# Attention and a mixture of experts in one kernel: products with V in two visits per head pair, full-array forms, and a reordered step table

## The chip, the cores and the metric

One core of a Trainium2 chip runs the whole program. The metric is the device time in microseconds of one execution. The matrix engine is called PE below (its weight loads PEld), the vector engine DVE, the scalar engine ACT, the general engine POOL, and SP issues most of the DMAs.

## The reference, cut to what matters

```python
q_rot, k_rot = rotate(q), rotate(k)                 # q, k, v: 2 batches, 8 heads, 576 tokens, 64 wide
scores = q_rot @ k_rot^T / sqrt(64)
attn = softmax(scores)                              # max subtracted; sum + 1e-9 below
x = (attn @ v) -> [1152, 512]                       # tokens by heads
logits = x @ w_gate; expert = argmax(logits)        # 8 experts, each with a capacity of 288 tokens
y = gate * relu(x_e @ w1[e]) @ w2[e]                # zero for a token that found no room
out = prelu(y @ w_in) @ w_out
```

All of it is float32.

## The kernel before

The program is one hand-ordered stream (a manual schedule): each engine runs its instructions in the order in which the code calls them, and waits are set by semaphores between engines. A step that stands late in one engine's queue cannot pass a step that stands before it.

Attention works on eight head pairs `j` (two heads of one batch each). The 576 tokens of a pair are four tiles of 128 and one rest of 64. Nine softmax steps make a pair: `(t, hh)` for four tiles and two heads, and `(4, 0)` for the two rests together. The loop `for n in range(10, ...)` counts slots, ten to a pair, so that `j, s = divmod(n, 10)`; one slot of the ten, `SCH["none"]`, has no softmax step. In each slot the letters of `SCH["seq"]` = `SATXPR` are gone through in order:

- **S**, `S_step`: the logits of a step (4 products, 8 for the rests; K is split in a high and a low half, so two stationary operands), into one of two `pss` buffers in PSUM; then DVE takes the row maximum (`nm`, line 308), and ACT the exponential into `P` (line 309), with the row sums in `ss`.
- **T**, `T_step`, two slots later (`lag`): PE transposes `P` into `pt` (and `pr`, which stays open for a pair), ACT or DVE (by the table `SCH["e"]`) copies it to `PT` and `PR`.
- **A**, `AV_steps(j - 1)`: the products of the former pair's `PT` and `PR` with `v`. Both heads have 64 columns, and each has its own half of the array's columns (a 128x64 form). Two halves of the tokens by five blocks of keys are ten pieces, one piece (two products, four records in the trace) in each slot. After five pieces the result is copied to `oT`.
- **X**, `xl_steps(j - 2)`: PE multiplies `oT` by `G` (an identity and the gate's weights), tile by tile, which gives tokens by features and the gate's logits; DVE scales both by the inverse row sums `ri` and writes `x_tok` and `lp`. The fifth tile has 64 columns, so it too is a 128x64 form.
- **P**, `prep_T`, `prep_rem`, `prep_X` for pair `j + 1`: PE transposes `hl` (K and Q of each head in two halves) into `pT`; a copy by DVE (K) or ACT (Q) makes `T`. `prep_rem` does so for the rests (`rb`, from the 64 rows of `remhl` that hold this batch: a form of 64 rows). `prep_X` issues two DMAs that swap halves of `T`.
- **R** for pair `j + 2`: `ropeA` on POOL (three operations for K, three for Q), `remA` (three), `ropeB` and `remB`: a cast on ACT and then a subtraction on POOL, which end in `hl` and `remhl`.

All of A, T, X and P take their PSUM tiles from one pool `ps1` with four buffers. After the letters come the slot's loads (`SCH["load"]`) and `hook(n)`, which starts the routing of the first batch at slot 53 (DVE, a few small products on PE, five indirect DMAs on POOL), `choose` at 61, the first expert's weights at 66, their splitting (ACT, POOL) from 68, and `make_xT` from 81. The last pair's products with V have the slots 80 to 89 to themselves, and its `xl_steps` come at 86 and 90. After that the expert and the feed-forward stages run.

Of the kernel before, what the change touches and what calls it, by code (L numbers as in the profile page):

```python
# [12 lines left out]
F32 = mybir.dt.float32  # L13
# [11 lines left out]
P = 128  # L25
# [20 lines left out]
SCALE = 1.0 / math.sqrt(D)  # L46
BIG = float(1 << 20)
LEFT, RIGHT = "left", "right"
SCH = {'xl': [0, 2], 'T': [1, 1, 1, 2], 'rem': 3, 'X': 4, 'rope': [0, 0, 7, 9, 3, 9], 'load': 9, 'none': 9, 'lag': 2, 'seq': 'SATXPR', 'e': [1, 1, 0, 0, 1, 0, 1, 0, 0, 0, 1, 0, 0, 0, 1, 0, 0, 0, 1]}


def rope_tables():
# [11 lines left out]
def attention(nc, tc, q, k, v, wg, tab, rtab, x_tok, lp, ident, idr, hook):  # L64
# [3 lines left out]
    with ExitStack() as ctx:  # L68
# [14 lines left out]
        vrem = cp.tile([P, 2, 8, 64], F32, name="vrem")  # L83
        G = cp.tile([P, 4, 144], F32, name="G")
        TR = cp.tile([P, 2, 3, 64], F32R, name="TR")
        nc.vector.memset(TR[:, :, 1].bitcast(F32), 0.0)
        state = {}

# [109 lines left out]
        def prep_rem(j):  # L198


            b, hp = divmod(j, NPAIR)
            h0 = 2 * hp
            st = state[j]
            rb = ps1.tile([P, 4, 64], F32R, tag="ps1", name=f"rb_{j}")
            sl = slice(64 * b, 64 * b + 64)
            for i in range(2):
                for hh in range(2):
                    nc.tensor.transpose(
                        rb[:, i * 2 + hh, :],
                        remhl[sl, i, h0 + hh].rearrange("p two d -> p (two d)"),  # L210
                        idr[sl, sl],
                    )
            flat = T_of(j, 1).rearrange("p h n -> p (h n)")[:, 512:640].rearrange("p (h n) -> p h n", h=2)
            for i, o in ((1, flat), (0, TR[:, j % 2, 0:3:2])):
                move(nc.scalar, i, o, rb[:, 2 * i : 2 * i + 2, :].bitcast(F32))
            st["X"] = pT.tile([P, 2, 576], F32R, tag="X", name=f"X_{j}")

        def prep_X(j, hh=None):
# [133 lines left out]
        def AV_steps(j):  # L352
            b, hp = divmod(j, NPAIR)
            st = state[j]
            PT, PR = st["PT"], st["PR"]
            oT = p2.tile([P, 576], F32, tag="oT", name=f"oT_{j}")
            st["oT"] = oT
            for half in range(2):
                ps = ps1.tile([P, 512], F32, tag="ps1", name=f"av_{j}_{half}")
                for kb in range(5):  # L360
                    for hh in range(2):
                        lhs = st["v"][:, hh, kb, :] if kb < 4 else vrem[:, b, 2 * hp + hh, :]
                        nc.tensor.matmul(  # L363
                            ps[64 * hh : 64 * hh + 64, 0:288],
                            lhsT=lhs,
                            rhs=(PT[:, hh, kb] if kb < 4 else PR)[:, half * 288 : half * 288 + 288],
                            start=(kb == 0),
                            stop=(kb == 4),
                        )
                    if kb == 4:  # L370
                        copy(17 + half, oT[:, half * 288 : half * 288 + 288], ps[:, 0:288])
                    yield

        def xl_steps(j, parts=((0, 3), (3, 5))):
            b, hp = divmod(j, NPAIR)
            st = state[j]
            oT = st["oT"]
            ri = p2.tile([P, 5, 2], F32, tag="ri", name=f"ri_{j}")
            nc.vector.tensor_scalar(ri, st["ssum"], 1e-9, None, op0=ALU.add)
            nc.vector.reciprocal(ri, ri)  # L380
            nc.vector.tensor_copy(ri[0:64, 4, 1:2], ri[64:128, 4, 0:1])
            for t0, t1 in parts:
                ps = ps1.tile([P, t1 - t0, 144], F32, tag="ps1", name=f"xl_{j}_{t0}")
                for t in range(t0, t1):
                    m = 128 if t < 4 else 64
                    nc.tensor.matmul(
                        ps[:m, t - t0, :], lhsT=oT[:, t * 128 : t * 128 + m], rhs=G[:, hp, :], start=True, stop=True
                    )
                last, later = j == B * NPAIR - 1 and t1 == 5, []
                for a, e, m in ((t0, min(t1, 4), 128), (4, t1, 64)):  # L390
                    if a >= e:
                        continue
                    rb = lambda n: ri[:m, a:e, :].unsqueeze(3).broadcast_to([m, e - a, 2, n])
                    src = ps[:m, a - t0 : e - t0]
                    nc.vector.tensor_tensor(
                        lp[:m, b, a:e, 2 * hp : 2 * hp + 2, :],
                        src[:, :, 128:144].rearrange("p t (h d) -> p t h d", h=2),
                        rb(8),
                        op=ALU.mult,
                    )  # L400
                    xo = x_tok[:m, b, a:e, hp * 128 : hp * 128 + 128].rearrange("p t (h d) -> p t h d", h=2)
                    xi = src[:, :, 0:128].rearrange("p t (h d) -> p t h d", h=2)
                    if not last:
                        nc.vector.tensor_tensor(xo, xi, rb(64), op=ALU.mult)
                        continue
                    later += [(xo[:, t - a, h], xi[:, t - a, h], ri[:m, t, h : h + 1]) for t in range(a, e) for h in range(2)]
                for xo, xi, scale in later:
                    nc.scalar.activation(xo, xi, AF.Copy, scale=scale)
                yield
            state.pop(j)  # L410
# [93 lines left out]
        for n in range(10, len(steps) + 11):  # L504
            j, s = divmod(n, 10)
            for what in SCH["seq"]:
                if what == "S" and n < len(steps):
                    if steps[n][1]:
                        S_step(j, *steps[n][1])
                if what == "T" and 0 <= n - LAG < len(steps):  # L510
                    jt, x = steps[n - LAG]
                    if x:
                        T_step(jt, *x)
                if what == "A" and 1 <= j <= NJ:
                    if s == 0:
                        avg = AV_steps(j - 1)
                    next(avg)
                if what == "X":
                    xs0 = SCH["xl"] if j < NJ else (1, 2)
                    if j >= 2 and s in xs0:  # L520
                        if s == xs0[0]:
                            xlg = xl_steps(j - 2)
                        next(xlg)
                if what == "P" and j + 1 < NJ:
                    for i, (x, y) in enumerate(zip(SCH["T"], ((1, 0), (1, 1), (0, 0), (0, 1)))):
                        if s == x:
                            prep_T(j + 1, *y, eng(i))
                    if s == SCH["rem"]:
                        prep_rem(j + 1)
                    if s == SCH["X"]:  # L530
                        prep_X(j + 1)
                        prep_sums(j + 1)
                if what == "R" and j + 2 < NJ:
                    at = SCH["rope"]
                    if s == at[0]:
                        ropeA(j + 2, Q, 1)
                    if s == at[1]:
                        ropeA(j + 2, Q, 0)
                    if s == at[4]:
                        remA(j + 2, Q)  # L540
                    if s == at[2]:
                        ropeB(j + 2, Q, 1)
                    if s == at[3]:
                        ropeB(j + 2, Q, 0)
                    if s == at[5]:
                        remB(j + 2, Q)
            if n in (NJ * 10 + 6, NJ * 10 + 10):
                if s:
                    xlg = xl_steps(NJ - 1, ((0, 2), (2, 5)))
                next(xlg)  # L550
            if s == SCH["load"] and j + 3 < NJ:
                prep_load(j + 3)
            if j == 1 and s == 4:
                for hh in range(2):
                    nc.sync.dma_start(
                        G[64 * hh : 64 * hh + 64, :, 128 + 8 * hh : 136 + 8 * hh],
                        wg.rearrange("(c hh p) e -> hh p c e", hh=2, p=64)[hh],
                    )
            if n == 10 * (NJ - 1) - 5:
                prep_ctx.close()  # L560
            hook(n, ps1)
# [284 lines left out]
def build(nc, tc, cap, q, k, v, wg, w1, w2, w_in, w_out, alpha, tab, rtab, out):  # L846
    assert 0 < cap <= W
    with ExitStack() as top:
# [110 lines left out]
        def hook(n, psum):  # L959
# [11 lines left out]
                nc.vector.tensor_scalar(nal, al, -1.0, None, op0=ALU.mult)  # L971
            if n > 16 and fill:
                nc.sync.dma_start(fill.pop(0), zero[0:96].unsqueeze(1).broadcast_to([96, 3, 512]))
            if n == 53:
                hook.r = gate.route(0, psum, "ps1")
            if n in (53, 54, 55, 56):
                next(hook.r)
            if n == 61:
                hook.c = gate.choose()
# [651 lines left out]
```

## Time and profile before

| | |
|---|---|
| time, median of 3 runs | 464.43 us (464.12 to 465.53) |
| the profiled execution: its own time | 468.51 us |
| its span, first to last instruction | 466.7 us |
| PE busy | 421.9 us (90% of the span) |
| DVE, ACT, POOL busy | 305.5, 216.1, 238.7 us |
| granted PE clock, mean | 0.982 |

A busy time is the union of an engine's instructions. Matmuls overlap in the array's pipeline, so what one costs is read from the distance between the starts of neighbours, not from its own duration. "[0.57 <-DVE nm L308]" behind an instruction says that its engine sat idle 0.57 us before it, and that line 308's `nm` on DVE ended that wait. "x4" stands for four instructions that were merged into one row.

### The profile page before, as it was taken

To read this page: it belongs to the slowest core of one execution; us is meant where nothing else is said; L and a number is where in the kernel's file an instruction comes from. 1 tells how busy PE (TensorE), PEld (TensorE's weight loads), DVE (VectorE), ACT (ScalarE), POOL (GpSimd) and SP (SyncE) were. 2 spreads that over 40 slices of the span, in tenths; PEclk is the share of its full clock that TensorE was granted. 3 is DMA by queue.
4 is the path that set the end of the run, shared out by engine and by line. 5 is a ranking of instruction groups with operands and counts; after the bars stand their busy time and mean duration, and the time that the engine had idled before them with its cause. 6 is when DMAs were issued, how large, how long until landed. Compare 5 with 4: busy or idle time off the path is not lost. (4 is left out here: it accounts for less than half of the span.)

```text
span 466.7 us, 8223 instructions
## 1 busy us (share of the span) xinstructions
PE 421.9 (90%) x2993; PEld 332.2 (71%) x2993; DVE 305.5 (65%) x563; ACT 216.1 (46%) x540; POOL 238.7 (51%) x280
## 2 busy tenths in 40 slices
PE   6789999999989999995878798998999899889993
PEld 3576666666666666695867798697689589758962
DVE  8996566574777464579489911139888797886321
ACT  2476767666665667342253331164424514432600
POOL 6578482864775334148645310047736745662532
PEclk9999999999999999999899898999999999999998
DMA  7422999604031624467466667940314045000012
GB/s 215 129 60 48 175 332 295 185 1 121 0 119 35 195 88 160 158 228 250 104 208 216 235 222 264 374 170 1 122 60 180 5 178 183 0 1 0 2 69 73
DMA packets 37329, 63.71 MB, mean 137 GB/s; under 512 B 9886, under 2 KB 16158, under 8 KB 37280
## 3 DMA queue, kind: packets, MB, share of 16 engines
q1 hardware_dynamic: 35424, 58.83, 39.7%
q0 software_dynamic: 1568, 3.95, 2.3%
q8 instruction: 25, 0.41, 0.4%
q10 hardware_dynamic: 288, 0.33, 0.2%
q14 instruction: 24, 0.20, 0.1%
HBM read 47.35 MB, written 11.65 MB: 126 GB/s over the span
## 5 line engine op out<-in xcount | busy, mean ns | idle before, releaser
L308 DVE TENSOR_REDUCE nm<-S 128x1 f32<-128x576 f32 x72 | 54.2, 755 | 45.0 <-PE S L299 27.7
L309 ACT ACTIVATE P<-S,nm 128x576 f32<-128x576 f32 x72 | 53.5, 742 | 52.6 <-DVE nm L308 51.0
L1124 PE MATMUL u_a<-yh,whl 128*128 128x256 f32 (+1 forms) x576 | 71.3, 284 | 6.1 <-ACT room L1134 5.7
L1124 PEld LDWEIGHTS u_a<-yh,whl 128*128 128x128 f32 x576 | 70.1, 188 | 7.4 <-ACT room L1134 6.4
L1136 DVE SCALAR_TENSOR_TENSOR room<-room,nal 128x256 f32<-128x256 f32 (+1 forms) x48 | 30.5, 637 | 30.9 <-ACT room L1134 30.8
L330 PEld LDWEIGHTS pt<-ident,P 128*128 128x128 f32 x256 | 27.0, 141 | 29.3 <-ACT P L309 6.8
L1026 POOL TENSOR_TENSOR whl<-wraw,whl 128x512 fp32r<-128x512 f32 x22 | 28.9, 1312 | 35.8 <-ACT whl L1025 32.7
L363 PE MATMUL av<-PT,v 128*64 128x288 f32 x256 | 44.7, 431 | 0.4 <-DVE PT L319 0.3
L1188 PE MATMUL acc<-whl,split_room 128*128 128x512 f32 x162 | 42.3, 396 | 2.2 <-DVE xs L1200 1.2
L330 PE MATMUL pt<-ident,P 128*128 128x128 f32 x256 | 41.5, 286 | 3.1 <-ACT P L309 2.9
L1025 ACT CAST whl<-wraw 128x512 fp32r<-128x512 f32 x22 | 14.5, 657 | 54.2 <-DVE wraw L1022 54.2
L1188 PEld LDWEIGHTS acc<-whl,split_room 128*128 128x128 f32 x162 | 29.7, 188 | 13.1 <-DVE xs L1200 2.9
L1142 POOL TENSOR_TENSOR g<-room,g 128x272 fp32r<-128x272 f32 (+2 forms) x21 | 17.7, 853 | 41.7 <-ACT g L1141 39.2
L299 PE MATMUL S<-T,T 128*128 128x288 f32 x112 | 36.1, 338 | 1.1 <-DVE T L178 1.1
L1188 PE MATMUL acc<-whl,g 128*128 128x512 f32 x126 | 32.9, 391 | 0.5 <-POOL whl L1026 0.5
L299 PE MATMUL S<-X,T 128*128 128x288 f32 x112 | 31.2, 293 | 0.0
L154 POOL TENSOR_TENSOR hl<-R,hl 128x512 fp32r<-128x512 f32 x12 | 15.4, 1287 | 30.6 <-ACT hl L153 30.5
L1142 POOL TENSOR_TENSOR split_room<-room,split_room 128x272 fp32r<-128x272 f32 (+2 forms) x27 | 24.6, 919 | 12.3 <-ACT split_room L1141 9.5
L1188 PEld LDWEIGHTS acc<-whl,g 128*128 128x128 f32 x126 | 23.5, 188 | 6.6 <-POOL whl L1026 0.9
L319 DVE COPY PT<-pt 128x512 f32<-128x512 f32 (+1 forms) x32 | 19.9, 623 | 12.2 <-PE pt L330 7.9
L319 ACT COPY PT<-pt 128x512 f32<-128x512 f32 (+1 forms) x48 | 26.0, 544 | 3.6 <-PE pt L330 3.4
L927 POOL TENSOR_TENSOR whl<-wraw,whl 128x512 fp32r<-128x512 f32 x12 | 15.9, 1329 | 22.3 <-ACT whl L924 22.3
(290 smaller groups left out, 925.4 us busy)
## 6 DMA issues: line engine op xcount, KB each, us to landing
wraw<-moe_w SPq DMA_DIRECT2D x16, 1024.0 KB, 6.3
wraw<-moe_w_out SPq DMA_DIRECT2D x3, 2048.0 KB, 8.1
x_disp<-zero SPq DMA_DIRECT2D x9, 576.0 KB, 8.0
wraw<-moe_w_in SPq DMA_DIRECT2D x2, 2048.0 KB, 10.1
X<-T SPq DMA_DIRECT2D x14, 288.0 KB, 4.1
room<-moe_w SPq DMA_DIRECT2D x3, 1024.0 KB, 6.5
out<-zero SPq DMA_DIRECT2D x4, 576.0 KB, 7.9
v<-v SPq DMA_DIRECT2D x8, 256.0 KB, 5.2
```

The source lines that it names most:

```text
L299: nc.tensor.matmul(ps[:, half, 0:288], lhsT=lhsT, rhs=rhs, start=(n == 0), stop=(n == len(terms) - 1),)
L308: nc.vector.tensor_reduce(nm, ps[:, :, 0:288], op=ALU.max, axis=AX.XY, negate=True)
L309: nc.scalar.activation(Pt.rearrange("p (a n) -> p a n", a=2), ps[:, :, 0:288], AF.Exp, bias=nm, scale=1.0, accum_out=st["ssum"][:, t, hh : ...
L319: (nc.vector.tensor_copy if SCH["e"][k] else nc.scalar.copy)(o, i)
L330: nc.tensor.transpose(ps[:, kb, :], Pt[:, at : at + 128], ident)
L363: nc.tensor.matmul(ps[64 * hh : 64 * hh + 64, 0:288], lhsT=lhs, rhs=(PT[:, hh, kb] if kb < 4 else PR)[:, half * 288 : half * 288 + 288], s ...
L927: eng.tensor_tensor(ht[:, 1, c], rt[:, c], ht[:, 0, c].bitcast(F32), op=ALU.subtract)
L1026: nc.gpsimd.tensor_tensor(ht[:, 1, c], hw.bitcast(F32), ht[:, 0, c].bitcast(F32), op=ALU.subtract)
L1124: nc.tensor.matmul(ps, lhsT=wt[:, a, c, (f % 4) * 128 : (f % 4) * 128 + 128], rhs=yh_[0][:, b, c, c0 + lo : c0 + hi], start=(c == 0 and i ...
L1136: nc.vector.scalar_tensor_tensor(A, Bn, nal[:, f : f + 1], A, op0=ALU.mult, op1=ALU.add)
L1142: nc.gpsimd.tensor_tensor(g_cols(g, 1, lo, mid), A[:, 0 : mid - lo], hi_.bitcast(F32), op=ALU.subtract)
L1188: nc.tensor.matmul(ps[:m], lhsT=g_cols(g, b, t * P, t * P + m), rhs=wt[:, a, c, :], start=(c == 0 and i == 0), stop=(c == 3 and i == 2),)
```

## The change

The step table is rewritten, and three forms are changed:

- `av` and `avl` say how many of the ten pieces a slot does: five at slot 4 and five at slot 8 of a pair; for the last pair five at slot 1 and five at slot 3 of its own slots.
- The slot without a softmax step is 8 instead of 9, so the rests' logits come at slot 9, and their transposes at slot 1 of the next pair instead of slot 0.
- `T`: the transposes of K's first head move from slot 1 to 0, those of Q's second head from slot 2 to 5. `rope`: `ropeA` for Q moves from slot 0 to 4. Two entries of `e` change places (tile 1: head 0 on ACT, head 1 on DVE).
- The last pair's `xl_steps` come at slots 83 and 85, those of the pair before it at 80 and 81.
- `oT` is two fixed tiles of 640 columns whose last 64 are set to zero, and `xl_steps` always takes 128 columns. `prep_rem` transposes all 128 rows of `remhl` (the unused ones are zeroed once) and reads the 64 columns that it wants.

```diff
-SCH = {'xl': [0, 2], 'T': [1, 1, 1, 2], 'rem': 3, 'X': 4, 'rope': [0, 0, 7, 9, 3, 9], 'load': 9, 'none': 9, ...
+SCH = {'xl': [0, 2], 'xll': [0, 1], 'end': [3, 5], 'route': 53, 'av': [0, 0, 0, 0, 5, 0, 0, 0, 5, 0], 'avl': [0, 5, 0, 5, 0, 0, 0, 0, 0, 0], 'T': [0, 1, 1, 5], 'rem': 3, 'X': 4, 'rope': [0, 4, 7, 9, 3, 9], 'load': 9, 'none': 8, ...
...
+        oTs = [cp.tile([P, 640], F32, name=f"oT{i}") for i in range(2)]
+        for z in oTs:
+            nc.gpsimd.memset(z[:, 576:640], 0.0)
+        nc.gpsimd.memset(remhl[64:128].bitcast(F32), 0.0)
...
-            rb = ps1.tile([P, 4, 64], F32R, tag="ps1", name=f"rb_{j}")
+            rb = ps1.tile([P, 4, 128], F32R, tag="ps1", name=f"rb_{j}")
...
-                        remhl[sl, i, h0 + hh].rearrange("p two d -> p (two d)"),
-                        idr[sl, sl],
+                        remhl[:, i, h0 + hh].rearrange("p two d -> p (two d)"),
+                        idr,
...
-                move(nc.scalar, i, o, rb[:, 2 * i : 2 * i + 2, :].bitcast(F32))
+                move(nc.scalar, i, o, rb[:, 2 * i : 2 * i + 2, sl].bitcast(F32))
...
-            oT = p2.tile([P, 576], F32, tag="oT", name=f"oT_{j}")
-            st["oT"] = oT
+            oT = st["oT"] = oTs[j % 2]
...
-                    m = 128 if t < 4 else 64
                     nc.tensor.matmul(
-                        ps[:m, t - t0, :], lhsT=oT[:, t * 128 : t * 128 + m], rhs=G[:, hp, :], start=True, stop=True
+                        ps[:, t - t0, :], lhsT=oT[:, t * 128 : t * 128 + 128], rhs=G[:, hp, :], start=True, stop=True
...
-                    next(avg)
+                    for _ in range(SCH["av" if j < NJ else "avl"][s]):
+                        next(avg)
...
-            if n in (NJ * 10 + 6, NJ * 10 + 10):
-                if s:
+            if n - NJ * 10 in SCH["end"]:
+                if n == NJ * 10 + SCH["end"][0]:
```

What this does to PE's queue at the beginning of pair 5 (slots 0 and 1; `av` are the pieces of pair 4, `xl` those of pair 3, `pT` the transposes of `hl` for pair 6: `pT_1` is K, `pT_0` is Q). Before, from the transposes of tile 3 on:

```order
L330 MATMUL pt_3_1_1539<-ident,P_3_1480 128x128 x4
L336 MATMUL pr_1419<-ident,P_3_1480 128x128
...
L363 MATMUL av_0_1568<-PT_1192,v_746 64x288 x2
L345 MATMUL pt_4_0_1571<-ident,P_4_1437 128x64 x4
...
L386 MATMUL xl_0_1591<-G,oT_1300 128x144 x3
...
L363 MATMUL av_0_1568<-PT_1192,v_746 64x288 x2
L190 MATMUL pT_1_0_1619<-idr,hl_6_1513 128x128 x4
L190 MATMUL pT_1_1_1626<-idr,hl_6_1513 128x128 x4
L190 MATMUL pT_0_0_1632<-idr,hl_6_1547 128x128 x4
```

The same stretch of the changed kernel:

```order
L334 MATMUL pt_3_1_1540<-ident,P_3_1478 128x128 x4
L340 MATMUL pr_1399<-ident,P_3_1478 128x128
...
L388 MATMUL xl_0_1572<-G,oT_162 128x144 x3
L194 MATMUL pT_1_0_1578<-idr,hl_6_1507 128x128 x4
...
L349 MATMUL pt_4_0_1599<-ident,P_4_1417 128x64 x4
...
L194 MATMUL pT_1_1_1615<-idr,hl_6_1507 128x128 x4
L194 MATMUL pT_0_0_1621<-idr,hl_6_1548 128x128 x4
```

The pieces of `av` are gone from here, the rests' logits (not shown) now stand directly ahead of the first of these rows, and one K transpose stands a slot earlier; the Q transposes keep their place behind the K ones.

POOL's queue in pair 5 (`A`, `B`, `R` are `ropeA`; `hl` is the end of `ropeB`; `x_disp` are the routing's five indirect DMAs). Before, behind `ropeA` of K:

```order
L128 TENSOR_TENSOR A_7_1603<-raw_7_1554,tabt 128x512
L129 TENSOR_TENSOR B_7_1604<-raw_7_1554,tabt 128x512
L131 TENSOR_TENSOR R_7_1605<-A_7_1603,B_7_1604 128x512
L128 TENSOR_TENSOR remA_1695<-rem,rtabt 64x256
...
L598 DMA x_disp<-x_tok,g_idx 10368x512 x5
L154 TENSOR_TENSOR hl_7_1832<-R_7_1599,hl_7_1832 128x8x64
```

The changed kernel, also behind `ropeA` of K:

```order
L132 TENSOR_TENSOR remA_1674<-rem,rtabt 64x256
...
L132 TENSOR_TENSOR A_7_1731<-raw_7_1555,tabt 128x512
L133 TENSOR_TENSOR B_7_1732<-raw_7_1555,tabt 128x512
L135 TENSOR_TENSOR R_7_1733<-A_7_1731,B_7_1732 128x512
L601 DMA x_disp<-x_tok,g_idx 10368x512 x5
L158 TENSOR_TENSOR hl_7_1825<-R_7_1587,hl_7_1825 128x8x64
```

The three operations of Q's `ropeA` now stand between the rests' rotation and the indirect DMAs.

## Rows read from the trace of the kernel before

**Rows 1.** Stretches, one per pair 1, 3 to 7, and the last slots; columns below.

The columns are: the stretch; its length; busy us (and instructions) of PE, PEld, DVE, ACT and POOL; PE's granted clock; the share of the DMA engines; GB/s. Pair 2 (54.04 to 75.33) is as long as pair 3.

```profile
34.07:54.04 19.97, 19.87 (x146) 13.49 (x147) 11.49 (x17) 13.45 (x34) 13.55 (x17) 1.00 0.45 63
...
75.33:96.62 21.29, 21.29 (x160) 14.65 (x158) 12.98 (x26) 14.19 (x35) 13.18 (x14) 1.00 0.62 185
96.62:118.52 21.90, 21.63 (x160) 14.68 (x158) 13.87 (x27) 14.20 (x35) 13.16 (x14) 1.00 0.24 65
118.52:141.85 23.33, 22.06 (x170) 15.16 (x169) 16.67 (x40) 14.15 (x35) 17.76 (x19) 1.00 0.24 74
141.85:163.33 21.48, 21.36 (x159) 14.65 (x158) 13.99 (x30) 14.49 (x37) 7.92 (x31) 1.00 0.39 108
163.33:182.84 19.51, 19.51 (x139) 12.90 (x138) 11.31 (x24) 13.91 (x34) 6.72 (x7) 1.00 0.24 71
182.84:194.92 12.08, 11.52 (x83) 6.43 (x83) 6.03 (x22) 4.88 (x12) 3.64 (x3) 1.00 0.48 166
```

**Rows 2.** Timeline of PE, slots 0 and 1 of pair 4: start, us, instruction.

```profile
98.53 1.00 PE L386 MATMUL xl<-G,oT 128*128 128x144 f32 x6
99.28 0.39 PE L299 MATMUL S<-T,T 128*128 128x288 f32 x1
...
99.64 0.29 PE L299 MATMUL S<-T,T 128*128 128x288 f32 x1
99.77 0.29 PE L299 MATMUL S<-X,T 128*128 128x288 f32 x1
99.99 0.71 PE L363 MATMUL av<-PT,v 128*64 128x288 f32 x4
100.63 1.22 PE L190 MATMUL pT<-idr,hl 128*128 128x128 f32 x12
101.68 0.36 PE L299 MATMUL S<-T,T 128*128 128x288 f32 x1
```

**Rows 3.** Timeline of PE, last slots: one piece alone, and two behind each other.

```profile
188.77 0.71 PE L363 MATMUL av<-PR,vrem 128*64 128x288 f32 x4
...
189.80 1.19 PE L363 MATMUL av<-PT,v 128*64 128x288 f32 x8
```

**Rows 4.** Timeline of PE, pair 3: tiles 3 and 4 of `xl`, and `rb`.

```profile
82.20 0.80 PE L386 MATMUL xl<-G,oT 128*128 128x144 f32 x4
82.93 0.54 PE L190 MATMUL pT<-idr,hl 128*128 128x128 f32 x4
...
85.33 0.50 PE L208 MATMUL rb<-idr,remhl 64*128 64x64 f32 x4
85.75 0.40 PE L299 MATMUL S<-T,T 128*128 128x288 f32 x1
```

**Rows 5.** Timelines of PE, ACT and POOL: from the rests' logits to `hl`.

```profile
93.00 0.38 PE L299 MATMUL S<-T,TR 128*128 128x288 f32 x1
...
95.21 0.74 ACT L309 ACTIVATE P<-S,nm 128x576 f32<-128x576 f32 x1 [0.57 <-DVE nm L308]
...
97.27 0.59 ACT L319 COPY PR<-pr 128x512 f32<-128x512 f32 x1
97.75 0.63 ACT L153 CAST hl<-R 128x512 fp32r<-128x512 f32 x1
...
98.46 1.28 POOL L154 TENSOR_TENSOR hl<-R,hl 128x512 fp32r<-128x512 f32 x1 [2.47 <-ACT hl L153]
```

**Rows 6.** Timeline of DVE: `ri` in pair 4 and in pair 7.

```profile
98.98 0.78 DVE L379 TENSOR_SCALAR ri<-ss 128x10 f32<-128x10 f32 x1
...
165.70 0.16 DVE L379 TENSOR_SCALAR ri<-ss 128x10 f32<-128x10 f32 x1
```

**Rows 7.** Timeline of POOL: one of the routing's five indirect DMAs.

```profile
136.17 0.98 POOL L598 DMA_INDIRECT x_disp<-x_tok,g_idx  x1 [0.31 <-issue]
```

**Rows 8.** Timeline of POOL, before pair 1: a wait, and a memset.

```profile
20.90 1.27 POOL L169 TENSOR_TENSOR remhl<-remR,remhl 64x256 fp32r<-64x256 f32 x1 [4.29 <-ACT remhl L168]
...
31.70 0.95 POOL L430 MEMSET vrem<- 128x1024 f32 x1
```

More of the change, by code (lines that the diff above doesn't have):

```diff
@@ L48 @@
 LEFT, RIGHT = "left", "right"
-SCH = {'xl': [0, 2], 'T': [1, 1, 1, 2], 'rem': 3, 'X': 4, 'rope': [0, 0, 7, 9, 3, 9], 'load': 9, 'none': 9, 'lag': 2, 'seq': 'SATXPR', 'e': [1, 1, 0, 0, 1, 0, 1, 0, 0, 0, 1, 0, 0, 0, 1, 0, 0, 0, 1]}
+SCH = {'xl': [0, 2], 'xll': [0, 1], 'end': [3, 5], 'route': 53, 'av': [0, 0, 0, 0, 5, 0, 0, 0, 5, 0], 'avl': [0, 5, 0, 5, 0, 0, 0, 0, 0, 0], 'T': [0, 1, 1, 5], 'rem': 3, 'X': 4, 'rope': [0, 4, 7, 9, 3, 9], 'load': 9, 'none': 8, 'lag': 2, 'seq': 'SATXPR', 'e': [1, 1, 0, 0, 1, 0, 0, 1, 0, 0, 1, 0, 0, 0, 1, 0, 0, 0, 1]}
 def rope_tables():
@@ L516, in attention @@
                         avg = AV_steps(j - 1)
-                    next(avg)
+                    for _ in range(SCH["av" if j < NJ else "avl"][s]):
+                        next(avg)
                 if what == "X":
-                    xs0 = SCH["xl"] if j < NJ else (1, 2)
+                    xs0 = SCH["xl"] if j < NJ else SCH["xll"]
                     if j >= 2 and s in xs0:
@@ L973, in hook @@
                 nc.sync.dma_start(fill.pop(0), zero[0:96].unsqueeze(1).broadcast_to([96, 3, 512]))
-            if n == 53:
+            if n == SCH["route"]:
                 hook.r = gate.route(0, psum, "ps1")
-            if n in (53, 54, 55, 56):
+            if SCH["route"] <= n < SCH["route"] + 4:
                 next(hook.r)
```

## The prediction

> **What bounds the kernel now.** I read the busy times by stretch first, one stretch per head pair. From pair 1 to pair 7 PE is busy 19.9 of 20.0 us, 21.3 of 21.3, 21.6 of 21.9, 22.1 of 23.3, 21.4 of 21.5 and 19.5 of 19.5, at a granted clock of 1.00 (the 2.4 GHz level), while DVE, ACT and POOL have 11 to 18 us of work in the same pairs [rows 1]. So in attention the time is what PE's queue takes, and a wait elsewhere costs nothing until PE waits for it. PE waits for something in pair 4 (0.27 us), pair 5 (1.27, the routing) and the last slots (0.56). Second, the timeline of PE, for what each step takes from its start to the start of the next one. Third, the timelines of ACT, DVE and POOL around the turn of a pair, to see how far ahead of PE they run: this is what decides how much of a shorter PE queue remains.
>
> **Products with V.** Two logits rows behind each other start 0.13 us apart (99.64, 99.77), but the piece of products with V behind them starts 0.22 later (99.99), so entering costs 0.09. From its start to the next engine step are 0.64 us (99.99 to 100.63) [rows 2]. Of these only 0.48 is work: a piece alone lasts 0.71, two pieces behind each other 1.19 [rows 3]. A piece by itself thus takes 0.73 us of the queue, five in one visit 0.09 + 0.64 + 4 x 0.48 = 2.65. Ten pieces cost 7.3 us, two visits 5.3: 2.0 us less for each of pairs 1 to 7, if logits followed by transposes have no gap of their own. No row of this loop shows that pair of neighbours; the bounds are no gap (0.13, as between logits) and the same 0.09, which in the six short slots of a pair gives back 0.54. I take none, since what follows the logits is then of the same form.
>
> **The other forms.** Tiles 3 and 4 of `xl` take 0.73 us (82.20 to 82.93) [rows 4], three full tiles 0.75 for six rows (98.53 to 99.28) [rows 2], so 0.125 a row and 0.50 for two full tiles: 0.23 less. `rb` takes 0.42 (85.33 to 85.75) [rows 4]; four full transposes of the same type, from twelve in 1.05 (100.63 to 101.68) [rows 2], 0.35: 0.07 less. The rests' transposes, a 64-row form, stood behind a piece and now stand between full forms: they enter at 0.09 of their own. A pair's queue becomes 2.0 + 0.23 + 0.07 - 0.09 = 2.2 us shorter.
>
> The Trainium skill speaks against `rb` (TensorEngine Tiling (Array Packing), Performance Considerations): a contraction of 64 or less should be tiled by rows, and widening it gives that up. By this, `rb` with twice the rows and columns would take twice its time, 0.42 us more in each of seven pairs, and the result would be 3 us later; the rows just read say that four transposes cost the same in either form.
>
> **The new wait of PE.** Moving the rests' logits to slot 9 puts them directly ahead of the next pair, without the pieces that stood between. From their start to `hl` of Q runs a chain: 2.21 us to the exponential's start (93.00 to 95.21), 0.74 for it, two copies on ACT at 0.48 each (97.27 to 97.75; the other has the same shape), 0.71 from the cast's start to POOL's (97.75 to 98.46), 1.28 on POOL: 5.9 us [rows 5]. ACT runs these in order, so PE's speed changes nothing in it. PE came to the first transpose of Q at 101.33 (100.63 and eight of the twelve), 8.33 us behind 93.00 [rows 2, 5]. Of these go four pieces (2.92) and four transposes of tile 3, now ahead of the rests' logits (0.35 by the transposes above); the 0.09 comes on top: 5.15. So PE, with all that is queued behind this transpose (the logits of slot 2 first), waits 0.75, with the signal's way 0.8 us in each pair that prepares another. The wait is bounded below by nothing, if ACT gets the cast done while its copies wait, and above by DVE: there the scaling of `xl`, the K copy and the next maximum stand in one line, and `ri` took 0.78 while POOL worked and 0.16 in pair 7 [rows 6]. In the new order `ri` comes about 1.3 us before POOL's `hl`, so I take the short one; with the long one the line ends 0.6 later and PE waits up to 0.5 more for the buffers of `ps1`.
>
> **POOL's queue.** Q's `ropeA` moves past the rests' rotation. An ordinary pair keeps POOL busy 13.2 us [rows 1] in about 19.9, and its result is wanted by a cast some 2.7 us later: hidden, and 1.28 us for each operation of slip if not. In pair 5 the routing's five DMAs, 1.29 us each with their gaps [rows 7], now stand behind it: `hl` of K for pair 7 comes at about 4.6 + 11.9 + 6.4 + 1.3 = 24.2 us behind the rests' logits of pair 4 (4.6 is where POOL starts in the chain above, 11.9 the ordinary work without `hl` of K). PE wants it at about 20.2 + 3.2 = 23.4, so it waits 0.8 to 1.5; I take 1.2, instead of the 0.8 at Q.
>
> **The start.** The zeroing on POOL has 64 x 2048 and twice 128 x 64 to write; 128 x 1024 took 0.95, so about 2.2 us. Behind it POOL's queue is late by that much, until a wait of 4.29 us for ACT [rows 8] that takes it up. Nothing; were the cover gone, 2.2.
>
> **The sum**, against the profiled execution (468.51 us, of which 466.7 span). Pair 1, without `xl`: 2.0 + 0.07 - 0.09 - 0.8 = 1.2. Pairs 2 and 3: 2.2 - 0.8 = 1.4 each. Pair 4: 1.4 and its old wait of 0.27, 1.7. Pair 5: 1.4 and 1.27, since the visit of 2.65 us now lies ahead of the routing's products, 2.7. Pair 6: 2.3 - 1.2 = 1.1. Pair 7 prepares nothing: 2.1, less a wait for ACT between 0 and 0.8, 1.7. The last slots: seven visits become two (5 x 0.25), two `xl` at 0.23, and the old wait of 0.56 disappears behind the `xt` transposes that now follow the visit: 2.2. Together 13.4 us, so 455.1 for that execution; the median of the runs shown stands to it as 464.43 to 468.51, which gives 451.1. The 272 us behind attention start when it ends and I expect them unchanged (1 us either way for their transfers).
>
> **Rivals.**
> - PE finds no new wait. For it: ACT has 14.2 us of work in a pair of 21.3 [rows 1]. Against it: the chain, which is order and not load. It adds 5 x 0.8, 1.2 and 0.4: 19.0 us, 445.6.
> - The gap before transposes remains and DVE's line is the longer one. For it: each transition into a smaller form has a gap. 7 x 0.54 and 6 x 0.45 less: 6.9 us, 457.6.
> - Slower: ACT paces every slot. With two logits buffers it may get nothing to do during the visits; then a pair is 5.3 us of visits plus ACT's 14.2 [rows 1], POOL's 1.28 and twice the 0.57 that ACT stood before an exponential [rows 5]: 21.9 instead of 21.3 in six pairs, less the last slots: about +1.5, 466. It decides from waits of more than some 3 us a pair. Against it: the logits of slots 3, 4 and 7 are queued ahead of a visit, so ACT has one or two exponentials and copies to do in it.
> - The Trainium skill has a rule that leads to the middle rival (the same page, PSUM Bottleneck): a faster PE can leave the emptying of PSUM as the bound. The trace shows three engines with a third of their time free, so by load it is not so here.
> - The change does not join the pieces: excluded by the order, five pieces in one row of PE's queue.
>
> **How the numbers follow.** The forecast, 448 to 454.5, has 0.55; no new wait 0.16; the middle one 0.19; no difference 0.04, where the new waits just eat the saving; ACT as the pace 0.06. The likeliest gives 451.1. The range takes in both neighbours with the 1 us of the later stages: 445.0 to 458.5; below and above lie about 0.05 and 0.13. A measurement of this kernel tells 0.3% (1.4 us) from no change: faster 0.90, same 0.04, slower 0.06.
>
> **What would show it.** Right: two visits per pair in PE's timeline, about 2.7 us to the next step, pairs 2 and 3 near 19.9 us, PE idle some 0.8 us before a `pT` transpose of Q at slot 1, ended by POOL's `hl`; in pair 6 before one of K. `rb` at 0.35. Wrong: pairs near 19.1 without that idle time (first rival); logits followed by a transpose 0.22 later instead of 0.13, or PE waiting there for DVE's `T` or `x_tok` (second); ACT without idle time before its exponentials in slots 5 to 7 and 9 to 1, and PE waiting for `P` (third).

## The result, and the profile after

The changed kernel takes 450.1 us (median of 4 runs, 448.3 to 450.9) against 465.0 us (4 runs, 464.1 to 466.3): ratio 0.969, 95% interval 0.965 to 0.973, or 14.9 us less. Its profiled execution took 450.14 us, its span is 448.1. PE is busy for 401.4 us, again 90% of the span.

The stretches of the changed kernel, columns as in [rows 1]: pairs 1 to 7, the last slots, then the experts' products from the first `h` on, the stretch from `mh` on, and the feed-forward part from `u_a` on.

```profile
34.64:54.14 19.50, 19.14 (x146) 15.55 (x147) 10.81 (x17) 12.60 (x32) 13.54 (x17) 0.91 0.48 66
54.14:73.84 19.70, 18.87 (x159) 15.54 (x158) 12.18 (x26) 13.86 (x35) 13.16 (x14) 1.00 1.00 322
73.84:93.54 19.70, 18.86 (x159) 15.52 (x158) 12.17 (x26) 14.04 (x35) 11.61 (x13) 1.00 0.76 230
93.54:113.94 20.40, 19.28 (x160) 15.54 (x158) 13.01 (x27) 13.97 (x35) 14.78 (x16) 1.00 0.26 70
113.94:134.45 20.51, 19.24 (x170) 15.77 (x168) 15.79 (x42) 14.17 (x36) 15.85 (x17) 1.00 0.21 66
134.45:155.07 20.62, 19.09 (x160) 15.49 (x158) 13.42 (x29) 14.07 (x35) 10.14 (x34) 1.00 0.47 131
155.07:173.18 18.11, 17.52 (x140) 13.86 (x139) 10.96 (x24) 13.62 (x33) 7.51 (x7) 1.00 0.18 58
173.18:183.41 10.23, 10.23 (x90) 7.44 (x89) 5.85 (x21) 5.31 (x14) 2.54 (x2) 1.00 0.75 251
183.41:252.28 68.87, 56.40 (x422) 54.53 (x421) 64.38 (x136) 28.79 (x57) 37.59 (x27) 0.99 0.68 227
252.28:283.04 30.76, 29.71 (x400) 26.52 (x399) 6.05 (x19) 6.81 (x22) 1.29 (x1) 0.96 0.85 300
283.04:448.10 165.06, 147.24 (x898) 124.33 (x898) 109.90 (x147) 61.23 (x169) 87.00 (x95) 0.98 0.21 79
```

Pair 3 went from 21.29 us [rows 1] to 19.70. It was all PE work before; now PE has 18.86 us of work and stands 0.84 us idle. The timeline of PE in the changed kernel shows a visit, the turn of the pair, and the wait of pair 6:

```profile
69.04 0.27 PE L340 MATMUL pr<-ident,P 128*128 128x128 f32 x1
69.24 2.16 PE L366 MATMUL av<-PT,v 128*64 128x288 f32 x16
...
71.82 0.66 PE L334 MATMUL pt<-ident,P 128*128 128x128 f32 x4
...
78.15 0.54 PE L194 MATMUL pT<-idr,hl 128*128 128x128 f32 x4 [0.81 <-POOL hl L158]
...
78.99 0.30 PE L303 MATMUL S<-X,T 128*128 128x288 f32 x1
79.12 0.60 PE L334 MATMUL pt<-ident,P 128*128 128x128 f32 x4
...
137.23 0.54 PE L194 MATMUL pT<-idr,hl 128*128 128x128 f32 x4 [1.26 <-POOL hl L158]
```

A visit of five pieces takes 2.58 us from its start to the next step (69.24 to 71.82), where five single pieces took 3.65 by [rows 2]. The row at 78.15 is the Q transpose behind which the prediction put a wait of 0.8 us; it stands in pairs 2 to 5 with 0.81, 0.81, 0.52 and 0.80. The row at 137.23 is K's in pair 6. A transpose follows logits after 0.13 us (78.99, 79.12), as one logits row follows another.

### The profile page after: what moved, and what is told of

It is laid out like the page before. It is cut to its first block, busy times and chain, and to the rows that moved or that the text cites. A ratio compares the mean times of both kernels' runs of the same rounds, so it can differ in the third digit from the quotient of the medians.

```text
span 448.1 us, 8240 instructions
## 1 busy us (share of the span) xinstructions
PE 401.4 (90%) x2999; PEld 337.7 (75%) x2999; DVE 304.8 (68%) x568; ACT 214.6 (48%) x540; POOL 240.9 (54%) x283
## 5 line engine op out<-in xcount | busy, mean ns | idle before, releaser
L334 PE MATMUL pt<-ident,P 128*128 128x128 f32 x256 | 39.1, 277 | 3.6 <-ACT P L313 2.4
L334 PEld LDWEIGHTS pt<-ident,P 128*128 128x128 f32 x256 | 29.8, 140 | 11.8 <-ACT P L313 4.1
L366 PE MATMUL av<-PT,v 128*64 128x288 f32 x256 | 34.6, 412 | 0.0
L1136 ACT ACTIVATE room<-u_a 128x256 f32<-128x256 f32 (+1 forms) x48 | 18.6, 388 | 17.2 <-PE u_a L1127 17.2
```

Source lines behind the costliest of these rows:

```text
L334: nc.tensor.transpose(ps[:, kb, :], Pt[:, at : at + 128], ident)
L366: nc.tensor.matmul(ps[64 * hh : 64 * hh + 64, 0:288], lhsT=lhs, rhs=(PT[:, hh, kb] if kb < 4 else PR)[:, half * 288 : half * 288 + 288], s ...
L1136: nc.scalar.activation(A, ps, AF.Relu)
```

## The experiments

The runs are named by their labels. Each group (e1 to e4, e5 to e8, e9 to e11, e12) shared a chip with its own runs of the kernel before. Their median for the kernel before was 464.6, 463.5, 468.1 and 466.7 us, so between groups only ratios are compared: a run's time over that of the kernel before on the same chip, with a 95% interval. The changed kernel's is 0.969. A pair's length is read from its trace.

### Visits and forms, one at a time

e1 changes the kernel before:

```diff
-                    next(avg)
+                    for _ in range((0, 0, 0, 0, 5, 0, 0, 0, 5, 0)[s] if j < NJ else 1):
+                        next(avg)
```

> The kernel before with the pieces of pairs 1 to 7 in two visits (slots 4 and 8) and nothing else changed; the last pair's pieces, the order and the forms stay. Theory of the prediction: each of seven pairs has a queue shorter by 2.0 us less 0.09 at the rests' transposes, and no new wait, because the rests' logits stay at slot 8 with a whole visit between them and the Q transposes: 13.4 us less, about 451.6 us, pairs 2 and 3 at 19.4 us. Rival (the new order is what makes the visits pay, since alone they let ACT run dry): PE waits for P or POOL's hl in each pair, less than half the gain, above 458 us.

459.6 us, ratio 0.988 (0.985 to 0.991): 5 us instead of 13. Pairs 2 and 3 take 20.98, not 19.4. Timeline of PE in this kernel, pair 3:

```profile
76.75 0.88 PE L190 MATMUL pT<-idr,hl 128*128 128x128 f32 x8 [0.36 <-ACT PR L319]
...
78.91 0.90 PE L386 MATMUL xl<-G,oT 128*128 128x144 f32 x4 [0.24 <-DVE T L176]
...
81.61 0.47 PE L208 MATMUL rb<-idr,remhl 64*128 64x64 f32 x4 [0.20 <-ACT T L174]
...
88.28 0.40 PE L299 MATMUL S<-T,T 128*128 128x288 f32 x1 [0.26 <-ACT P L309]
```

None of these is a wait for data that the step multiplies: the first three want one of the four `ps1` buffers, which the copies named on the right have to empty, the last one a logits buffer.

e2 has the forms alone, the changed kernel with the tables of before:

```diff
-'xll': [0, 1], 'end': [3, 5], ... 'T': [0, 1, 1, 5], ... 'rope': [0, 4, 7, 9, 3, 9], ... 'none': 8, ... 'e': [1, 1, 0, 0, 1, 0, 0, 1, 0, ...
+'xll': [1, 2], 'end': [6, 10], ... 'T': [1, 1, 1, 2], ... 'rope': [0, 0, 7, 9, 3, 9], ... 'none': 9, ... 'e': [1, 1, 0, 0, 1, 0, 1, 0, 0, ...
-'av': [0, 0, 0, 0, 5, 0, 0, 0, 5, 0], 'avl': [0, 5, 0, 5, 0, 0, 0, 0, 0, 0]
+'av': [1] * 10, 'avl': [1] * 10
```

> The kernel before with the three full-array forms alone (xl of the fifth tile, rb, the fixed oT tiles); tables and pieces as before. Theory: 0.23 + 0.07 us per pair in seven pairs, about 2 us less, 462.9 us, rb at 0.35 to 0.37 and xl of tiles 3 and 4 at 0.4 to 0.5. Rival (widening a 64-row contraction costs its size): rb 0.84, about 3 us more, 468 us.

460.6 us, ratio 0.992 (0.989 to 0.995): 4.0 us less, twice the expected, and pairs 2 and 3 at 20.73 and 20.74, so 0.55 a pair instead of 0.30. Timeline of PE before, and with the forms alone:

```profile
85.12 0.27 PE L336 MATMUL pr<-ident,P 128*128 128x128 f32 x1
```

```profile
82.00 0.66 PE L388 MATMUL xl<-G,oT 128*128 128x144 f32 x4
82.40 0.55 PE L194 MATMUL pT<-idr,hl 128*128 128x128 f32 x4
...
84.60 0.27 PE L340 MATMUL pr<-ident,P 128*128 128x128 f32 x1
84.62 0.54 PE L212 MATMUL rb<-idr,remhl 128*128 128x128 f32 x4
85.00 0.37 PE L303 MATMUL S<-T,T 128*128 128x288 f32 x1
```

Before, `rb` started 0.21 us behind `pr` (85.12, and 85.33 in [rows 4]); as a full form it starts 0.02 behind it. That entry of 0.19 was not in the sum. `rb` itself takes 0.38 instead of 0.42, and the two tiles of `xl` 0.40 (82.00 to 82.40) instead of 0.73: together 0.56.

The Trainium skill says of such switches only that "Mode switching requires drain" (TensorEngine Tiling (Array Packing), Key Properties). The rows agree and give a price: 0.19 us into this 64-row form, 0.25 for a separate 128x64 visit.

### The new order without the visits, and the visits without the new order

e3 changes the changed kernel:

```diff
-'av': [0, 0, 0, 0, 5, 0, 0, 0, 5, 0]
+'av': [1, 1, 1, 1, 1, 1, 1, 1, 1, 1]
```

> The changed kernel with the pieces of pairs 1 to 7 one to a slot again (last pair as changed). Theory: visits cost 2.0 us more in each of seven pairs, but three pieces now stand between the rests' logits and the Q transposes, so the waits for POOL's hl (0.8 us in pairs 2 to 5, 1.26 in pair 6) go: +14.0 - 4.5 = +9.5, about 459.6 us. Rival (these waits hide no time of the queue): +14 us, 464 us.

469.3 us, ratio 1.010 (1.006 to 1.013): slower than the kernel before, and beyond both expectations. PE's wait for `T` in pair 3, a stretch of pair 5 (columns as above), and one operation of DVE and one of POOL ahead of that stretch:

```profile
82.34 0.51 PE L194 MATMUL pT<-idr,hl 128*128 128x128 f32 x4 [0.88 <-DVE T L180]
```

```profile
135.00:147.00 12.00, 10.95 (x56) 6.93 (x55) 4.79 (x14) 5.48 (x13) 5.03 (x5) 0.57 0.25 93
```

```profile
131.10 1.20 DVE L670 TENSOR_TENSOR r_d<-r_lg,r_mx 128x40 f32<-128x40 f32 x1
```

```profile
130.97 1.27 POOL L132 TENSOR_TENSOR A<-raw,tabt 128x512 f32<-128x512 f32 x1
```

The wait for POOL's `hl` is gone as expected, but another of 0.88 us stands in its place, ended by the copy that empties a `ps1` buffer. A likely reason, from the code and not tested by itself, is that the result of the single pieces holds one of the four buffers through five slots. Pairs 2 and 3 take 21.78. Without the wait that is 20.90, and the changed kernel without its own 18.89: the price of the visits, 2.0 us a pair, was right. Pair 5 took 30.0 us, because PE, after a wait of 2.2 us for the routing's `g_oh`, ran at a granted clock of 0.57, close to the 1.2 GHz level, for 12 us. What made `g_oh` late is taken up with e5.

e9 is the opposite: the old order, with visits, forms and last slots as changed.

```diff
-'T': [0, 1, 1, 5], ... 'rope': [0, 4, 7, 9, 3, 9], ... 'none': 8, ... 'e': [1, 1, 0, 0, 1, 0, 0, 1, 0, ...
+'T': [1, 1, 1, 2], ... 'rope': [0, 0, 7, 9, 3, 9], ... 'none': 9, ... 'e': [1, 1, 0, 0, 1, 0, 1, 0, 0, ...
```

> The changed kernel with the order of before: the slot without a step, the places of hl's transposes, of Q's rotation and the table of copies as they stood; visits, forms and last slots as changed. Theory (the order is there to keep the four PSUM buffers and ACT's line from eating the visits): pairs 2 and 3 at 20.98 - 0.55 = 20.4 instead of 19.7, about 5 us more, 455 us. Rival (with the shorter forms the old order would do as well, as the prediction's own sum would have it, since it has no wait for hl): pairs 2 and 3 at 19.1, 446.5 us.

462.9 us, ratio 0.987 (0.984 to 0.991). Pairs 2 and 3 take 20.90, more even than the theory's 20.4. The same waits for `ps1` buffers stand there as in e1 (PE, pair 3):

```profile
79.10 0.88 PE L194 MATMUL pT<-idr,hl 128*128 128x128 f32 x8 [0.36 <-ACT PR L323]
...
81.24 0.76 PE L388 MATMUL xl<-G,oT 128*128 128x144 f32 x4 [0.23 <-DVE T L180]
```

e7 restores one part of the order alone in the changed kernel, the places of the transposes of `hl`:

```diff
-'T': [0, 1, 1, 5]
+'T': [1, 1, 1, 2]
```

> The changed kernel with the transposes of hl where they stood before (three at slot 1, one at slot 2). Theory (the four PSUM buffers that all transposes share, emptied by DVE and ACT, are why grouping alone gave 5 us): PE waits for K's and Q's copies in slots 1 and 2, some 0.8 us more in each of six pairs, about 455 us. Rival (the place of these transposes is immaterial, the other moves count): 450 us.

455.5 us, ratio 0.984 (0.980 to 0.988); pairs 2 and 3 at 20.52 and 20.51, 0.8 longer, with PE idle 0.93 us before the Q transposes until DVE's `T` has emptied a buffer (pair 3):

```profile
81.59 0.51 PE L194 MATMUL pT<-idr,hl 128*128 128x128 f32 x4 [0.93 <-DVE T L180]
```

Us per pair (pairs 2 and 3), all with the new forms:

| | one piece a slot | two visits |
|---|---|---|
| old order | 20.74 | 20.90 |
| new order | 21.78 | 19.70 |

In the old order the visits bring nothing (with the old forms, in e1, 0.3), the new order without visits costs 1.0, and both together save 1.0. Of the 1.2 us that the order is worth beside the visits, the transposes' places are 0.8; the other 0.4 were not taken apart. That the buffers are the cause is read from the copies that end PE's waits; no run had more of them.

### Is PE's wait for `hl` what limits a pair now?

e4 changes the changed kernel:

```diff
-'T': [0, 1, 1, 5]
+'T': [0, 1, 2, 5]
```

> The changed kernel with Q's first transposes at slot 2 instead of 1. Theory: PE's 0.8 us wait for POOL's hl goes in pairs 2 to 5, pair 6 keeps its 1.26 before K: 3.2 us less, about 446.9 us, pairs 2 and 3 at 18.9 us. Rival (DVE's line of scaling, K copy and maximum is as late): PE waits there for a buffer or the next P, under 1 us less, 449.5 us.

450.9 us, ratio 0.970 (0.967 to 0.974): nothing gained, pairs 19.66 and 19.88. PE at the turn of pair 3:

```profile
75.43 0.51 PE L194 MATMUL pT<-idr,hl 128*128 128x128 f32 x4
76.68 0.40 PE L303 MATMUL S<-T,T 128*128 128x288 f32 x1 [0.73 <-ACT P L313]
```

The wait for `hl` is gone from pairs 2, 3 and 5, and the logits behind it wait for the exponential that empties their buffer.

e5, from the changed kernel:

```diff
-'rope': [0, 4, 7, 9, 3, 9]
+'rope': [0, 0, 7, 9, 3, 9]
```

> The changed kernel with Q's rotation on POOL back at slot 0. Theory: in pair 5 it no longer stands ahead of the routing's DMAs, so PE's wait of 1.26 us for hl of K in pair 6 goes and the usual 0.8 at Q takes its place: 0.5 us less, about 449.7 us; pairs 2 and 3 stay at 19.7. Rival: POOL now works beside DVE's scaling of xl (ri 0.78 instead of 0.16) and DVE's line becomes the late one: pairs 2 to 6 longer by about 0.5, 452.5 us.

453.2 us, ratio 0.979 (0.973 to 0.986). The 1.26 us of pair 6 became 0.80, as the theory had it, and pair 6 takes 19.6. But pair 5 grew from 20.5 to 25.5 us. DVE, POOL and PE there, then the stretch behind:

```profile
121.96 1.28 DVE L670 TENSOR_TENSOR r_d<-r_lg,r_mx 128x40 f32<-128x40 f32 x1
123.27 1.19 DVE L672 SCALAR_TENSOR_TENSOR r_cand<-r_d,g_w 128x40 f32<-128x40 f32 x1
124.50 0.20 DVE L675 TENSOR_REDUCE r_mc<-r_cand 128x5 f32<-128x40 f32 x1
124.73 1.07 DVE L676 TENSOR_TENSOR g_oh<-r_cand,r_mc 128x40 bf16<-128x40 f32 x1
```

```profile
121.90 1.29 POOL L132 TENSOR_TENSOR A<-raw,tabt 128x512 f32<-128x512 f32 x1
123.13 1.28 POOL L133 TENSOR_TENSOR B<-raw,tabt 128x512 f32<-128x512 f32 x1
124.49 1.26 POOL L135 TENSOR_TENSOR R<-A,B 128x512 f32<-128x512 f32 x1
```

```profile
125.86 0.23 PE L688 MATMUL r_ps<-g_oh,g_idb 128*128 128x32 bf16 x3 [1.42 <-DVE g_oh L676]
```

```profile
128.00:134.00 6.00, 5.96 (x28) 5.60 (x30) 3.20 (x12) 3.55 (x8) 3.12 (x6) 0.51 0.20 75
```

Three DVE operations on 40 columns end with the POOL operation that ran when they came; the reduction between them takes its usual 0.20. In the changed kernel Q's rotation is not there yet, and POOL runs the rests' shorter operations (0.72 us each):

```profile
122.98 0.20 DVE L670 TENSOR_TENSOR r_d<-r_lg,r_mx 128x40 f32<-128x40 f32 x1
...
124.09 0.42 DVE L676 TENSOR_TENSOR g_oh<-r_cand,r_mc 128x40 bf16<-128x40 f32 x1
```

The Trainium skill has such a hold as a lock on ports that DVE shares with POOL, held for a whole instruction, for a DVE operation with two inputs in SBUF, and not for a reduction (SBUF — State Buffer, Who interferes with whom). The rows agree (1.28 us for `r_d`, 0.20 for the reduction).

So the move of Q's rotation to slot 4, which the prediction entered as a cost of up to 1.5 us in pair 6, keeps PE here from a wait of 1.42 us in pair 5 and from six us at about half the clock behind it. It does so by what falls together, not by the slot as such. In e3, with the rotation at slot 4, the same three operations end with Q's rotation on POOL (`r_d`, shown there, took 1.20 us), and PE waits 2.2 us for `g_oh`. In e6 below, with the rotation at slot 0, POOL begins it 4.4 us earlier than in e5, `r_d` takes 0.33 us, and PE does not wait for `g_oh`.

e6, from e5:

```diff
-'rope': [0, 0, 7, 9, 3, 9]
+'rope': [0, 0, 7, 8, 3, 8]
```

> As the run before, and the casts and subtractions of Q's and of the rests' second step at slot 8 instead of 9, where ACT stands idle for 2.8 us during the visit. Theory (ACT's line from the rests' exponential on is what PE waits for, first through hl, and through P once hl is out of the way): both waits go, since casts of 0.64 and 0.40 us leave that line: 0.8 in pairs 2 to 5 and 1.26 in pair 6, 4.5 us less, about 445.6 us, pairs 2 and 3 at 18.9. Rival (the pace is set elsewhere, as by DVE's copies): less than 1 us, 449.5 us.

449.4 us, ratio 0.972 (0.965 to 0.978): pairs 2 and 3 at 19.57, 0.13 less, which is the rival; pair 5 takes 21.3. The wait for `hl` is gone from pairs 2 and 3, and PE now waits for DVE (pair 3):

```profile
77.74 0.66 PE L334 MATMUL pt<-ident,P 128*128 128x128 f32 x4 [0.40 <-DVE T L180]
```

e11 is e6 with the late zeroing of the next section and

```diff
-'e': [1, 1, 0, 0, ...
+'e': [1, 0, 0, 0, ...
```

> The run with casts at slot 8 (449.4 us), with the late zeroing, and with the copy of K's second head on ACT instead of DVE. Theory (PE's 0.4 us wait for T of DVE in pairs 2 to 5 is the last of the three lines there): 1.6 + 0.6 us less, about 447.2 us, pairs 2 and 3 at 19.2. Rival (ACT's line is as late once it has that copy too): pairs unchanged or longer, 449 us or more.

459.2 us, ratio 0.979 (0.976 to 0.983): the rival. Pairs take 19.87, in pair 4 22.15, and PE waits for ACT's copy of `pr`:

```profile
80.38 0.66 PE L331 MATMUL pt<-ident,P 128*128 128x128 f32 x4 [0.70 <-ACT PR L320]
```

POOL's chain, ACT's line and DVE's copies thus end within a few tenths of each other at the turn of a pair; taking one away leaves the next. No version here beats the changed kernel measurably.

### The start

e10 changes the changed kernel:

```diff
-        for z in oTs:
-            nc.gpsimd.memset(z[:, 576:640], 0.0)
-        nc.gpsimd.memset(remhl[64:128].bitcast(F32), 0.0)
...
+        for z in oTs:
+            nc.gpsimd.memset(z[:, 576:640], 0.0)
+        nc.gpsimd.memset(remhl[64:128].bitcast(F32), 0.0)
         remB(1, Q)
```

> The changed kernel with its two zeroings moved on POOL's queue into its wait of 4.3 us before remhl, from about 3.6 us to about 17 us. Theory (the zeroing of 1.80 us costs the start 0.57 us, not through POOL's queue but because DVE's operations of that time stand still until it ends): pair 1 starts at 34.1 or before, about 0.6 us less, 449.5 us. Rival (POOL's queue was the way, or the start is hidden): no difference, 450.1 us.

454.1 us on a chip with 468.1 for the kernel before: ratio 0.969 (0.966 to 0.972), as the changed kernel's; 0.6 us cannot be told here by the time. The traces tell it: POOL and DVE of the changed kernel, then DVE of this one.

```profile
3.87 1.80 POOL L89 MEMSET remhl<- 64x2048 f32 x1
```

```profile
4.13 1.59 DVE L444 CAST swap<-ident 128x64 fp32r<-128x64 f32 x1
```

```profile
4.13 0.34 DVE L441 CAST swap<-ident 128x64 fp32r<-128x64 f32 x1
```

The cast ends at 5.72, just behind the memset's end at 5.67. Without that, pair 1 starts at 33.99 instead of 34.64.

### The last slots, and the kernel before once more

e8 gives the kernel before the new last slots alone. e12 is the kernel before, unchanged.

```diff
-                    next(avg)
+                    for _ in range(1 if j < NJ else (0, 5, 0, 5, 0, 0, 0, 0, 0, 0)[s]):
+                        next(avg)
...
-                    xs0 = SCH["xl"] if j < NJ else (1, 2)
+                    xs0 = SCH["xl"] if j < NJ else (0, 1)
...
-            if n in (NJ * 10 + 6, NJ * 10 + 10):
-                if s:
+            if n in (NJ * 10 + 3, NJ * 10 + 5):
+                if s == 3:
```

> The kernel before with the new last slots alone: the last pair's products with V in two visits at slots 81 and 83, xl_steps at 80 and 81, 83 and 85; pairs 0 to 7 as before. Theory: the last slots take 10.3 us instead of 12.1, and the stages behind attention get shorter too, because the tokens of the second batch are sent earlier and PE no longer waits 1.8 us for xs, nor runs at a lower clock behind that wait: 1.8 + 2.8, about 460.0 us. Rival (only the last slots): 462.8 us.

460.8 us, ratio 0.995 (0.992 to 0.998): 2.7 us less, where the theory had 4.6 and the rival 1.8. In its trace the last slots (from the rests' logits to the first `h`) are 1.0 us shorter, not 1.8, and the stretch from `mh` to `u_a` falls to 30.65 us. Pair 5 was 1.5 us longer in this execution, at a clock of 0.83 for ten us.

> The kernel before once more, unchanged, for a second profiled execution. Theory (the first one, 3.5 us above the median of its runs, lost its excess behind attention, to waits for transfers and to the clock): attention ends within 0.5 us of the first one's 194.92, the stages behind it take about 268 us instead of 271.8, and the pairs repeat to 0.1 us. Rival (these stages always take 271.8 in this kernel, so the changed kernel's 264.7 is 7 us of real gain): 271 to 272.5 us again.

468.4 us (8 runs) beside 466.7 (9 runs of the same kernel), ratio 1.003 (1.000 to 1.007): this is how far identical kernels come apart. The pairs repeat within 0.1 us but one (pair 6, 0.2), attention ends at 194.65 (194.92), and 270.1 us follow instead of 271.8, neither theory's figure. The stretches behind attention in e12, the one from `mh` on in e8, and PE's wait for `xs` in e12 and in e8:

```profile
194.65:267.83 73.18, 62.06 (x421) 59.57 (x420) 60.03 (x128) 28.52 (x57) 37.17 (x27) 0.91 0.66 217
267.83:300.12 32.29, 28.66 (x401) 25.21 (x399) 6.34 (x20) 7.00 (x23) 1.30 (x1) 1.00 0.84 291
```

```profile
264.77:295.42 30.65, 29.20 (x399) 25.99 (x398) 5.59 (x19) 6.75 (x22) 1.30 (x1) 0.97 0.87 301
```

```profile
281.71 0.40 PE L1258 MATMUL xs<-ident,xs 32*128 32x32 f32 x4 [1.96 <-DMA xs<-x_disp]
```

```profile
277.02 0.40 PE L1259 MATMUL xs<-ident,xs 32*128 32x32 f32 x4 [0.41 <-DMA xs<-x_disp]
```

Two things lie behind attention, then. From the first `h` to `mh` all eight kernels of the first two groups took 68.2 to 69.7 us, and the four of the last two 73.2 to 73.6, whatever their order: that goes with the chip and not with the kernel. The first profiles of before and after (73.8 and 68.9) differ by as much. On which chips they ran is not on record, but on the chips of the last two groups the kernel before took 73.2 there and the changed kernel with the late zeroing 73.2, so this difference is not put down to the change. From `mh` to `u_a` the four profiles with the old last slots took 32.3 to 34.2 us, with waits of 1.7 to 2.3 for `xs`; the ten with the new ones 30.6 to 32.8, nine of them with waits of at most 0.82. The two ranges overlap; on the one chip that had both (e1 to e4) they are 34.1 and 34.2 against 30.6 and 31.1. Of e8's 2.7 us, about 1.7 are left for this stretch when the last slots' 1.0 is taken off. About 2 us there are the change's. Why the load of `xs` lands earlier was not settled.

## Why the prediction was right, and where it was not

The time, 451.1 against 450.1, was right, and so was the picture of a pair. Two sums of it were wrong and nearly cancelled: attention gave 1.9 us less than forecast, and the stages behind it about 2 us that the forecast did not have. That the total came out within 1 us is in this part luck. Gain in us, stretch by stretch, of the two profiled executions:

| | predicted | measured |
|---|---|---|
| start | 0 | -0.6 |
| pair 1 | 1.2 | 0.5 |
| pairs 2 and 3, each | 1.4 | 1.6 |
| pair 4 | 1.7 | 1.5 |
| pair 5 | 2.7 | 2.8 |
| pair 6 | 1.1 | 0.9 |
| pair 7 | 1.7 | 1.4 |
| last slots | 2.2 | 1.9 |
| attention | 13.4 | 11.5 |
| behind it | 0 | 7.1, of which about 2 the change's |

- **Visits.** 2.65 us for five pieces; 2.58 and an entry of 0.09 were measured at slot 4, and 2.0 us a pair from the run with single pieces. Only the second visit enters dearer than the sum has it: at slot 8 no logits stand ahead, and it starts 0.20 us behind `pr`, where a full form starts 0.02 behind it (e2). No gap opened between logits and transposes. Right.
- **Forms.** 0.30 predicted, 0.55 measured in the old order. The step that failed is the price of `rb`: it was read from its own start, and its entry, 0.19 us behind `pr`, was left out. The two tiles of `xl` cost 0.40 instead of the assumed 0.50. That full forms cost no more than 64-row ones held.
- **The wait for `hl`.** 0.8 predicted, 0.81 measured; 1.2 in pair 6, 1.26 measured. Place, cause and size were right. What it means was not: the sum treated it as the one thing between PE and a pair of 18.9 us, but without it another wait stands there (e4, e6).
- **The order.** The working held that PE's queue was the only limit before, so that the visits would pay in any order and the new one only cost a wait. By that the visits with the old order should have been the better kernel. They are not (20.90 us a pair against 19.70): with a shorter queue the `ps1` buffers become late. The rival on emptied PSUM was set aside because three engines had a third of their time free; that share did not show it, as four buffers bound by order, not by load.
- **POOL's queue.** Q's rotation past the rests was priced as a cost in pair 6 (right) and hidden elsewhere. In e5 the old place costs 5 us in pair 5, since it falls beside the routing's operations on DVE; e3 and e6 show that this depends on when POOL comes to it. Pair 5's gain, 2.8 us for 2.7, was so in part luck: the sum let the old wait of 1.27 us go because a visit now lies ahead of the routing's products, but in e5 that visit lies there too, and PE waits 1.42 us for `g_oh`.
- **The rivals.** "No new wait" fell with the rows of `hl`; the gap before transposes did not open, though its other half, DVE's line, ends a wait of 0.49 us in pair 4. "ACT paces every slot" fell too: ACT did run out of work during a visit, as this rival had it (2.81 us in the row below), but PE waited for no `P` in pairs 2 to 6. ACT in the changed kernel, behind the second visit:

```profile
74.44 0.74 ACT L313 ACTIVATE P<-S,nm 128x576 f32<-128x576 f32 x1 [2.81 <-DVE nm L312]
```

- **Start and pair 1.** The zeroing was "hidden" behind POOL's wait of 4.29 us [rows 8]. That wait does hide it on POOL's queue; the 0.6 us went through DVE, which the argument did not look at. In pair 1 no wait for `hl` arose, but PE ran at a granted clock of 0.53 from 36.4 to 40.0. In the run with the late zeroing, with 1.00 there, pair 1 is 1.1 us shorter up to its rests' logits.
- **Behind attention.** Expected unchanged within 1 us; about 2 us shorter, through the new last slots. With the 11.5 this gives 13.5 of the 14.9 us between the medians, whose interval reaches from 12.7 to 16.2.

## What to carry to other kernels

When the engine that bounds a loop gets a shorter queue, look next at what its steps borrow (PSUM buffers, logits buffers) and at the order in which they are returned, not at the busy share of the engines that return them: here the same visits were worth 0 or 2 us a pair, by the order of the other steps, and of that above all by the places of two of the four groups of `hl`'s transposes. Price a change of array form with its entry, read from the start of the step before it to its own. And ask of each operation moved or added on POOL which DVE operations run beside it, not only what stands behind it on POOL; the answer can change with every other move.

## What the runs showed of the hardware

- A DVE operation that meets a running POOL operation can stand until that one ends: 1.28 instead of 0.20 us for `r_d`, 1.59 instead of 0.34 for a cast beside a memset; a reduction did not.
- PE's clock can fall to its lower level after short waits in an otherwise full stretch: behind 1.42 and 0.88 us in pair 5 (0.51 over six us), behind 2.2 us (0.57 over twelve). It need not: at the start of pair 1, waits of 1.31 and 0.36 us were followed by 1.00 in e5 and in e10, waits of 1.30 and 0.36 by 0.53 in the changed kernel. So e5's pair 5, with 1.9 us more of waits than the changed kernel's, took 5 us longer.
- The stretch behind attention, in the same code, took about 4 us longer on two chips than on two others (73.2 to 73.6 against 68.2 to 69.7, one profile per kernel, a single one on one of the chips).
